# Fixed engine orders from one plan, padded feature buffers scaled by one GpSimd operation, and later query products in a fused linear-attention and gated-MLP kernel

## The chip, the cores and the metric

One core of a Trainium2 chip. The metric is the device time of one execution in microseconds (us). Medians are quoted, and the traces, whose spans are shorter than the device time by 1.7 us, decide where a microsecond went.

## The reference, cut to what matters

```python
x = A_x                                   # 1 x 2048 x 640, bf16
xn = layernorm(x)
q, k, v = split(xn @ wqkv)                # 32 heads of 20
phi_q = concat(softmax(q @ w_phi), softmax(-(q @ w_phi)))     # 40 features per head
phi_k = ...the same of k
kv, z = sum over s of phi_k * v, sum over s of phi_k          # per head
attn = (phi_q @ kv) / (phi_q @ z + 1e-6) @ wo
gated = (silu(xn @ w1) * (xn @ w3)) @ w2                      # F = 1536
return x + attn + gated
```

The kernel works on 16 tiles of 128 rows in 4 chunks. For every key or query tile TensorE projects (L431/L432 below), ScalarE takes exp of +p and -p, VectorE sums per head (reduction) and inverts (reciprocal), and the exponentials are scaled by the inverse (the *feature product*). A gate/up unit is two TensorE products into two banks of PSUM (the memory into which TensorE writes), a tanh on ScalarE, the gate operation `gs = (tanh + 1) * gate` on VectorE, which frees a bank, a copy of the up product on ScalarE and a last product on GpSimd.

## The kernel before

A small list scheduler, `Plan`, works out an order from assumed durations. Before the change only the first part was emitted in that order; the rest went through the framework's own scheduler, held by pins.

```python
def features(t, key, engines):            # before; cut
    ...
    def tail():                           # heads 30 and 31, on VectorE
        pinned[key, t] = nc.vector.tensor_mul(
            out=box["phi"][:, NB - 1, :, 0 : 2 * Dh]..., in0=box["e"][:, :, n * Dh : D]..., in1=box["r"][:, :, n:H, None]...)
    for sgn, eng in enumerate(engines):   # heads 0 to 29, +p and -p: two operations of 600 elements
        def mul(sgn=sgn, eng=eng):
            (nc.vector if eng == "DVE" else nc.gpsimd).tensor_mul(out=box["phi"][:, 0 : NB - 1, sgn, ...], ...)
...
def ln_stats(t, k=None, parts=(0, 1)):    # k: the operation that it must follow
...
b = plan.op("DVE", dve_us(512), gs, deps=[a, ab["gs"]], frees=[ug, ab["th"]])      # gate operation
...
for t in range(4, 8):
    ln_stats(t, ("g", 0, t - 2))          # statistics of chunk 1 behind gate operations
...
    if 8 <= t < 15:
        Q(t - 8)                          # query tiles 0..6 beside the key tiles
KV(NST - 2)
fill(2.2)                                 # one gate/up unit
KV(NST - 1)                               # last key/value product
...
order = plan.run()
with tc.manual_schedule(engines=...):
    ...                                   # first part only
kv_constants()
for o in order:                           # the rest: framework's scheduler, SyncE pinned
    if o["n"] >= early:
        ins = o["fn"]()
        ...
```

The softmax here doesn't subtract the row's maximum and nothing guards it: scores larger than these inputs give would overflow.

## Time and profile before

| | before |
|---|---|
| device time, median (all 6 runs before the prediction) | 274.4 us (274.02 to 276.53) |
| span in the trace | 272.65 us |
| TensorE at its own pace | 260.26 us |
| TensorE lost: start-up (first 14 us) / 20 to 27 us / gate banks 27 to 135 us / end of keys / after 145 us | 4.64 / 0.28 / 2.56 / 1.10 / 0 us |
| after the last matmul | 2.73 us |

How to read it: TensorE's matmuls have a fixed pace by shape (512 columns 0.216 us, 320 columns 0.136 us), so whatever lies between two matmul starts beyond the pace is lost time, and the span is pace, losses and the two ends. A *gate-bank* loss is a wait of TensorE for a bank that a gate operation frees late. The prediction shows the lines.

### The profile page before, as it was taken

The numbers are of one execution on the slowest core, as the hardware profiler recorded it, in microseconds if no ns is written. First come the engines' busy times: TensorE is split into PE (matmuls) and PEld (weight loads), VectorE is DVE, ScalarE is ACT, GpSimd is POOL, SyncE is SP. The second block draws the span as 40 slices with busy tenths as digits, with TensorE's granted clock in tenths as the row PEclk, the third lists the DMA queues.
The fourth block names the chain that finished last, engine by engine and source line by source line (L and its number), as shares of the span: only waits on it lengthen the run. The fifth ranks groups of instructions, "written<-read, shape, count | busy, mean of one in ns | idle before, by whom it ended". The sixth has DMA issues, their size and how long they took to land.

```text
span 272.6 us, 5218 instructions
## 1 busy us (share of the span) xinstructions
PE 264.9 (97%) x1964; PEld 164.2 (60%) x1964; DVE 184.8 (68%) x347; ACT 126.9 (47%) x285; POOL 138.9 (51%) x154
## 2 busy tenths in 40 slices
PE   7999999899999998999989999999999999999995
PEld 2545555455555665666645577766665765657775
DVE  5525899976866999799997828876567563444321
ACT  3668676557667776677754404233234133121000
POOL 6133567994568576988885422434632553112000
PEclk9999999999999999999999999999999999999999
DMA  7999927700280016706169456289814746412251
GB/s 197 312 220 306 255 80 177 268 2 0 96 99 0 2 54 172 209 37 174 68 162 331 117 137 169 103 222 288 206 49 145 168 144 188 115 50 64 82 73 48
DMA packets 70265, 38.11 MB, mean 140 GB/s; under 512 B 49632, under 2 KB 68192, under 8 KB 70240
## 3 DMA queue, kind: packets, MB, share of 16 engines
q1 hardware_dynamic: 69664, 37.42, 51.4%
q10 hardware_dynamic: 576, 0.36, 0.5%
q8 instruction: 15, 0.25, 0.4%
q14 instruction: 10, 0.08, 0.1%
HBM read 12.81 MB, written 12.98 MB: 95 GB/s over the span
## 4 chain that ended last, share of the span: by engine, by line
PE 77%; DVE 13%; issue 4%; DMA 2%; ACT 2%; SPq 0%; ACTq 0%; DVEq 0%
PE bank L633 30%; PE bank L798 19%; PE bank L432 16%; PE bank L811 8%; DVE xn L339 2%; DVE ks L490 2%; DMA wv<-in_A_wqkv_dram 2%; PE rtbank L708 2%; DVE gs L654 2%; DVE qs L490 2%; DVE stats L294 1%; PE bank L590 1%; DVE kr L501 1%; ACT ek L481 1%; DVE phi_124 L507 1%
## 5 line engine op out<-in xcount | busy, mean ns | idle before, releaser
L677 POOL TENSOR_TENSOR hT<-gs,up 128x512 bf16<-128x512 bf16 x48 | 56.1, 1171 | 77.1 <-DVE gs L654 30.2
L633 PE MATMUL bank<-xnT,w_107 128*128 128x512 bf16 x240 | 59.6, 379 | 2.1 <-DVE gs L654 2.1
L633 PE MATMUL bank<-xnT,w_108 128*128 128x512 bf16 x240 | 59.6, 379 | 0.0
L432 PEld LDWEIGHTS <-xnT 128*128 128x128 bf16 x480 | 45.8, 98 | 21.0 <-issue 1.0
L798 PE MATMUL bank<-w_109,hT 128*128 128x320 bf16 (+2 forms) x396 | 55.0, 295 | 0.0
L798 PEld LDWEIGHTS <-hT 128*128 128x128 bf16 x396 | 38.2, 98 | 15.7
L649 ACT ACTIVATE th<-bank 128x512 bf16<-128x512 f32 x48 | 28.7, 599 | 39.8 <-PE bank L633 39.8
L654 DVE SCALAR_TENSOR_TENSOR gs<-th,bank 128x512 bf16<-128x512 bf16 x48 | 32.5, 678 | 19.4 <-ACT th L649 18.9
L481 ACT ACTIVATE eq<-bank 128x320 bf16<-128x320 f32 x64 | 22.9, 439 | 44.1 <-PE bank L432 33.7
L633 PEld LDWEIGHTS <-w_108 128*128 128x128 bf16 x240 | 23.5, 98 | 28.3
L672 ACT ACTIVATE up<-bank 128x512 bf16<-128x512 f32 x48 | 28.7, 597 | 25.0 <-PE bank L633 25.0
L633 PEld LDWEIGHTS <-w_107 128*128 128x128 bf16 x240 | 22.9, 98 | 24.1 <-issue 2.8
L490 DVE TENSOR_REDUCE qs<-eq 128x64 f32<-128x1280 bf16 x16 | 23.7, 1482 | 12.0 <-ACT eq L481 12.0
L490 DVE TENSOR_REDUCE ks<-ek 128x64 f32<-128x1280 bf16 x16 | 23.6, 1473 | 8.7 <-ACT ek L481 8.7
L432 PE MATMUL bank<-wv,xnT 128*128 128x320 bf16 x160 | 24.7, 299 | 0.8 <-DMA wv<-in_A_wqkv_dram 0.7
L811 PE MATMUL bank<-wo,oT 128*128 128x320 bf16 (+2 forms) x165 | 24.6, 294 | 0.0
L432 PE MATMUL bank<-wkphi,xnT 128*128 128x320 bf16 x160 | 24.3, 299 | 0.0
L432 PE MATMUL bank<-wqphi,xnT 128*128 128x320 bf16 x160 | 24.3, 299 | 0.0
L737 DVE TENSOR_SCALAR den<-rtbank 128x18 f32<-128x18 f32 (+1 forms) x32 | 4.9, 173 | 27.9 <-PE rtbank L708 27.9
L481 ACT ACTIVATE ek<-bank 128x320 bf16<-128x320 f32 x64 | 23.0, 439 | 0.6 <-PE bank L432 0.4
L825 DVE TENSOR_TENSOR res<-bank,xr 128x320 bf16<-128x320 f32 (+2 forms) x33 | 14.5, 470 | 10.4 <-PE bank L811 10.4
L811 PEld LDWEIGHTS <-oT 128*128 128x128 bf16 x165 | 14.9, 97 | 4.9
(117 smaller groups left out, 264.9 us busy)
## 6 DMA issues: line engine op xcount, KB each, us to landing
xr<-in_A_x_dram SPq DMA_DIRECT2D x4, 640.0 KB, 6.1
out_dram<-res SPq DMA_DIRECT2D x15, 160.0 KB, 2.5
w_107<-in_B_w_dram SPq DMA_DIRECT2D x4, 480.0 KB, 6.7
w_108<-in_B_w_dram SPq DMA_DIRECT2D x4, 480.0 KB, 7.5
w_109<-in_B_w_dram SPq DMA_DIRECT2D x1, 1920.0 KB, 8.4
xg<-in_A_x_dram SPq DMA_DIRECT2D x9, 160.0 KB, 4.0
wv<-in_A_wqkv_dram SPq DMA_DIRECT2D x2, 400.0 KB, 5.8
wo<-in_A_wo_dram SPq DMA_DIRECT2D x1, 800.0 KB, 5.5
```

Source lines behind the costliest of these rows:

```text
L339: ins = nc.vector.tensor_scalar(out=xn[c][:, i, :], in0=xg[c][:, i, :], scalar1=mv[:, t, 0:1], scalar2=rstd[:, t : t + 1], op0=ALU.subtrac ...
L432: nc.tensor.matmul(o["ps"][:], xnT[:, c, t * P : (t + 1) * P], w[:, c, 320 * half : 320 * half + 320], start=(c == 0), stop=(c == KD - 1),)
L481: nc.scalar.activation(out=box["e"][:, sgn, 320 * half : 320 * half + 320], in_=o["ps"][:], func=AF.Exp, scale=1.0 - 2.0 * sgn,)
L490: nc.vector.reduce_sum(out=box["s"][:].rearrange("p a h -> p (a h)"), in_=box["e"][:].rearrange("p a (h d) -> p (a h) d", d=Dh), axis=AX.X,)
L633: nc.tensor.matmul(o["ps"][:], w[:, k, fi * P : (fi + 1) * P], xs[:, k, :], start=(k == 0), stop=(k == KD - 1))
L649: nc.scalar.activation(out=box["th"][:], in_=og["ps"][:], func=AF.Tanh, scale=0.5)
L654: pinned["g", c, fi] = nc.vector.scalar_tensor_tensor(out=box["gs"][:], in0=box["th"][:], scalar=1.0, in1=og["ps"][:], op0=ALU.add, op1=AL ...
L672: nc.scalar.activation(out=box["up"][:], in_=ou["ps"][:], func=AF.Copy, scale=0.5)
L677: lambda: nc.gpsimd.tensor_mul(out=hT[c][:, fi, :], in0=box["gs"][:], in1=box["up"][:]),
L798: nc.tensor.matmul(o["ps"][:], hT[c][:, fi, ti * P : (ti + 1) * P], w2[:, fi, lo:hi], start=(fi == 0), stop=False,)
L811: nc.tensor.matmul(o["ps"][:], oT[c][:, k, ti * P : (ti + 1) * P], wo_of[0][:, k, lo:hi], start=False, stop=(k == KD - 1),)
L825: nc.vector.tensor_tensor(out=box["res"][:, lo:hi], in0=o["ps"][:], in1=xr[c][:, ti, lo:hi], op=ALU.add)
```

## The change

Its intent: take small work off VectorE (the tails), halve the number of GpSimd feature products, fix the order of every engine by a plan that also models the SBUF port shared by VectorE and GpSimd, and place query products, attention and residual loads later.

```diff
+exps = [acts.tile([P, 2, HB * NB, Dh], bf, ...) for i in range(4)]     # padded to 33 heads, pads zero
+recs = [acts.tile([P, 2, HB * NB], f32, ...) for i in range(2)]
 # features()
-        def tail(): ...                                    # two heads on VectorE
-        for sgn, eng in enumerate(engines): def mul(...)   # 2 x 600 elements
+        muls = [plan.op("POOL", 2.5, mul(0, 2, nc.gpsimd), ...)]            # 1320 elements, one operation
+        # key tiles 14 and 15: one operation of 1320 on VectorE
 # Plan
+            done = (max(t, port) if o["port"] else t) + o["dur"]
+            if o["port"]:
+                port = done
 # gate operation
-        b = plan.op("DVE", dve_us(512), gs, ...)
+        b = plan.op("DVE", dve_us(512), gs, ..., soon=0.4)   # taken up to 0.4 us ahead of its turn
 # five gate/up units: last product on VectorE
-        return "POOL"
+        return "DVE" if 22 <= n < 32 and n % 2 else "POOL"
-        ln_stats(t, ("g", 0, t - 2))
+        ln_stats(t)
-        if 8 <= t < 15:
+        if 8 <= t < 14:
             Q(t - 8)
     KV(NST - 2)
+    Q(6)
     fill(2.2)
     KV(NST - 1)
 # last stage: RT, ATT, OT (attention of a tile) and residual loads placed later (cut)
-    kv_constants()
-    ...                                                    # framework's scheduler
+        kv_constants()
+        for o in order:                                    # whole kernel in the plan's order
+            if o["n"] >= early:
+                o["fn"]()
```

The change also alters the plan's assumptions for a few operations (the landing of the second chunk's load from 19.0 to 21.5 us, some durations, and an advance such as the gate's for two other operations).

More of the change, by code (lines that the diff above doesn't have):

```diff
@@ L17, in __init__, with op @@
         self.ops = []
-    def op(self, eng, dur, fn, deps=(), takes=None, frees=(), after=0.0, lat=0.0, soon=0.0):
+    def op(self, eng, dur, fn, deps=(), takes=None, frees=(), after=0.0, lat=0.0, soon=0.0, port=False):
         o = dict(eng=eng, dur=dur, fn=fn, deps=[d for d in deps if d is not None], takes=takes,
-                 frees=list(frees), after=after, lat=lat, soon=soon, n=len(self.ops), end=None, open=0)
+                 frees=list(frees), after=after, lat=lat, soon=soon, port=port or eng == "POOL", n=len(self.ops), end=None, open=0)
         for f in o["frees"]:
@@ L36, in run @@
         left = len(self.ops)
+        port = 0.0
         def ready(o):
@@ L66, in run @@
                 ring.remove(min(ring))
-            o["start"], o["end"] = t, t + o["dur"] + o["lat"]
-            free[o["eng"]] = t + o["dur"]
+            done = (max(t, port) if o["port"] else t) + o["dur"]
+            if o["port"]:
+                port = done
+            o["start"], o["end"] = t, done + o["lat"]
+            free[o["eng"]] = done
             queue[o["eng"]].remove(o)
@@ L151 @@
     phis = [acts.tile([P, NB, 2, 64], bf, name=f"phi{i}") for i in range(5)]
+    exps = [acts.tile([P, 2, HB * NB, Dh], bf, name=f"exp{i}") for i in range(4)]
+    recs = [acts.tile([P, 2, HB * NB], f32, name=f"rec{i}") for i in range(2)]
     kva, kvb = (kvpool.tile([P, 512], f32, name=n, tag="kv", bufs=2) for n in ("kva", "kvb"))
@@ L247, in kv_constants @@
             nc.gpsimd.memset(phi[:, :, :, HB * Dh : 64], 0.0)
-            nc.gpsimd.memset(phi[:, NB - 1, :, 2 * Dh : HB * Dh], 0.0)
+        for e in exps:
+            nc.gpsimd.memset(e[:, :, H:, :], 0.0)
+        for r in recs:
+            nc.gpsimd.memset(r[:, :, H:], 0.0)
         for q in range(2):
@@ L253, in kv_constants @@
         )
-    pinned = {}
     pin_of = {}
-    def order_after(ins, other):
-        tc.add_manual_dep(
-            ins.ins, other.ins.name,
-            mybir.DependencyInfo(mybir.DependencyClass.NoSync, mybir.DependencyReason.DATA), reason="order",
-        )
     plan = Plan(dict(bank=6, five=4, half=2, pair=4, phi=5, om=4, kv=2, th=3, gs=3, up=3, hT=3, big=3))
@@ L277 @@
     rstd = consts.tile([P, NST], f32, name="rstd")
-    arrive = [2.2, 2.6, 3.0, 3.4] + [19.0] * 4
+    arrive = [2.2, 2.6, 3.0, 3.4] + [21.5] * 4
     stats_of = {}
@@ L293, in fn @@
             for h in parts:
-                ins = nc.vector.bn_stats(out=stats[:, t, h, :], in_=xg[c][:, i, h * 320 : (h + 1) * 320])
-                if k is not None:
-                    order_after(ins, pinned[k])
+                nc.vector.bn_stats(out=stats[:, t, h, :], in_=xg[c][:, i, h * 320 : (h + 1) * 320])
             if parts[-1] == 1:
@@ L338, in fn @@
         def fn():
-            ins = nc.vector.tensor_scalar(
+            nc.vector.tensor_scalar(
                 out=xn[c][:, i, :], in0=xg[c][:, i, :], scalar1=mv[:, t, 0:1], scalar2=rstd[:, t : t + 1],
@@ L342, in fn @@
             )
-            if k is not None:
-                order_after(ins, pinned[k])
-        apply_of[t] = plan.op("DVE", 0.5, fn, deps=[rstd_of[t], *deps], frees=[xg_of[c]])
+        apply_of[t] = plan.op(
+            "DVE", dve_us(D, 4), fn, deps=[rstd_of[t], *deps], frees=[xg_of[c]], port=True, soon=1.5 if c == 1 else 0.0
+        )
         return apply_of[t]
@@ L369, in LN_out @@
             "SP", 0.5,
-            lambda: [nc.sync.dma_start(out=xn_d[c][:].rearrange("(t p) d -> p t d", p=P), in_=xn[c][:])],
+            lambda: nc.sync.dma_start(out=xn_d[c][:].rearrange("(t p) d -> p t d", p=P), in_=xn[c][:]),
             deps=ds, frees=[a], lat=3.5,
@@ L374, in tr @@
         def tr():
-            pinned["xnT", c] = ins = nc.sync.dma_start_transpose(
+            nc.sync.dma_start_transpose(
                 out=xnT[:, :, 512 * c : 512 * c + 512], in_=xn_d[c][:]
             )
-            return [ins]
         xt = plan.op("SP", 2.5, tr, deps=[st], lat=3.0)
@@ L462, in features @@
         box = {}
-        exps = []
+        done = []
         w, ready = (wkphi, wphi_ready["k"]) if key == "k" else (wqphi, wphi_ready["q"])
         def al():
-            box["e"] = work.tile([P, 2, D], bf, name="e" + key, tag="pair", bufs=4)
+            box["e"] = exps.pop(0)
+            exps.append(box["e"])
         def alp():
@@ L481, in ex @@
                     nc.scalar.activation(
-                        out=box["e"][:, sgn, 320 * half : 320 * half + 320], in_=o["ps"][:],
-                        func=AF.Exp, scale=1.0 - 2.0 * sgn,
+                        out=box["e"][:, sgn, 16 * half : 16 * half + 16, :],
+                        in_=o["ps"][:].rearrange("p (h d) -> p h d", d=Dh), func=AF.Exp, scale=1.0 - 2.0 * sgn,
                     )
-                exps.append(plan.op("ACT", act_us(320), ex, deps=[u, ea], frees=[u]))
+                done.append(plan.op("ACT", act_us(320), ex, deps=[u, ea], frees=[u]))
@@ L488, in red @@
         def red():
             box["s"] = small.tile([P, 2, H], f32, name=key + "s", tag="ks", bufs=2)
-            nc.vector.reduce_sum(
-                out=box["s"][:].rearrange("p a h -> p (a h)"),
-                in_=box["e"][:].rearrange("p a (h d) -> p (a h) d", d=Dh), axis=AX.X,
-            )
-        last = plan.op("DVE", dve_us(2 * D), red, deps=exps)
-        pa = plan.alloc("phi", alp)
-        muls = []
-        def rec():
-            box["r"] = small.tile([P, 2, H], f32, name=key + "r", tag="kr", bufs=2)
-            nc.vector.reciprocal(out=box["r"][:], in_=box["s"][:])
@@ L503, in features @@
-        last = plan.op("DVE", dve_us(2 * H, 0.15), rec, deps=[last])
-        n = HB * (NB - 1)
-        def tail():
-            pinned[key, t] = nc.vector.tensor_mul(
-                out=box["phi"][:, NB - 1, :, 0 : 2 * Dh].rearrange("p a (h d) -> p a h d", d=Dh),
-                in0=box["e"][:, :, n * Dh : D].rearrange("p a (h d) -> p a h d", d=Dh),
-                in1=box["r"][:, :, n:H, None].to_broadcast([P, 2, H - n, Dh]),
-            )
-        muls.append(plan.op("DVE", dve_us(2 * (H - n) * Dh), tail, deps=[last, pa], frees=[ea]))
@@ L514, in features @@
-        for sgn, eng in enumerate(engines):
-            def mul(sgn=sgn, eng=eng):
-                (nc.vector if eng == "DVE" else nc.gpsimd).tensor_mul(
-                    out=box["phi"][:, 0 : NB - 1, sgn, 0 : HB * Dh].rearrange("p b (h d) -> p b h d", d=Dh),
-                    in0=box["e"][:, sgn, 0 : n * Dh].rearrange("p (b h d) -> p b h d", h=HB, d=Dh),
-                    in1=box["r"][:, sgn, 0:n, None]
-                    .to_broadcast([P, n, Dh])
-                    .rearrange("p (b h) d -> p b h d", h=HB),
-                )
-            muls.append(
-                plan.op(eng, dve_us(n * Dh) if eng == "DVE" else 1.22, mul, deps=[last, pa], frees=[ea])
-            )
+            nc.vector.reduce_sum(out=box["s"][:], in_=box["e"][:, :, 0:H, :], axis=AX.X)
@@ new lines, in features, with rec, mul, fn @@
+        last = plan.op("DVE", dve_us(2 * D), red, deps=done)
+        def rec():
+            box["r"] = recs.pop(0)
+            recs.append(box["r"])
+            nc.vector.reciprocal(out=box["r"][:, :, 0:H], in_=box["s"][:])
+        last = pin_of[key, t] = plan.op("DVE", dve_us(2 * H, 0.15), rec, deps=[last])
+        pa = plan.alloc("phi", alp)
+        def mul(at, n, eng):
+            def fn():
+                eng.tensor_mul(
+                    out=box["phi"][:, :, at : at + n, 0 : HB * Dh].rearrange("p b a f -> p a b f"),
+                    in0=box["e"][:, at : at + n].rearrange("p a (b h) d -> p a b (h d)", h=HB),
+                    in1=box["r"][:, at : at + n, :, None].to_broadcast([P, n, HB * NB, Dh]),
+                )
+            return fn
@@ new lines, in features @@
+        if engines == ("DVE", "DVE"):
+            muls = [plan.op("DVE", dve_us(1320), mul(0, 2, nc.vector), deps=[last, pa], frees=[ea], port=True)]
+        elif engines[1] == "POOL":
+            muls = [plan.op("POOL", 2.5, mul(0, 2, nc.gpsimd), deps=[last, pa], frees=[ea])]
+        else:
+            muls = [
+                plan.op("POOL", 1.3, mul(0, 1, nc.gpsimd), deps=[last, pa], frees=[ea]),
+                plan.op("DVE", dve_us(660), mul(1, 1, nc.vector), deps=[last, pa], frees=[ea], port=True),
+            ]
@@ L528, in features @@
         return muls, pa, box
     def K(t):
-        phik_of[t], phik_a[t], _ = features(t, "k", ("POOL", "POOL" if t < NST - 1 else "DVE"))
-        pin_of["k", t] = phik_of[t][0]
+        phik_of[t], phik_a[t], _ = features(t, "k", ("POOL", "POOL") if t < NST - 2 else ("DVE", "DVE"))
     def Q(t, engines=("POOL", "POOL")):
@@ L567, in fn @@
                 )
-        KV_of[t] = plan.op("PE", pe_us(NB, 63), fn, deps=phik_of[t] + V_of[t], frees=[phik_a[t]])
+        KV_of[t] = plan.op("PE", 0.032 * NB, fn, deps=phik_of[t] + V_of[t], frees=[phik_a[t]])
     FSPANS = (
@@ L653, in gs @@
         def gs():
-            pinned["g", c, fi] = nc.vector.scalar_tensor_tensor(
+            nc.vector.scalar_tensor_tensor(
                 out=box["gs"][:], in0=box["th"][:], scalar=1.0, in1=og["ps"][:], op0=ALU.add, op1=ALU.mult
             )
-        b = plan.op("DVE", dve_us(512), gs, deps=[a, ab["gs"]], frees=[ug, ab["th"]])
+        b = plan.op("DVE", dve_us(512), gs, deps=[a, ab["gs"]], frees=[ug, ab["th"]], soon=0.4)
         pin_of["g", c, fi] = b
@@ L692, in fn @@
                 )
-            kvm_of.append(plan.op("DVE", dve_us(63 * (b1 - b0)), fn, deps=[KV_of[NST - 1]]))
+            kvm_of.append(plan.op("DVE", dve_us(63 * (b1 - b0)), fn, deps=[KV_of[NST - 1]], soon=1.0))
     rt_of = {}
@@ L714, in RT @@
             u = plan.op(
-                "PE", pe_us(b1 - b0, 63), fn, deps=[kvm_of[half], pqT_of[pair]], takes="kv", frees=[pqT_a[pair]]
+                "PE", 0.032 * (b1 - b0), fn, deps=[kvm_of[half], pqT_of[pair]], takes="kv", frees=[pqT_a[pair]]
             )
@@ L989 @@
             gates[0][0]()
+        if t < 2:
+            RT(t + 3)
+            ATT(t + 3)
+            OT(t + 3)
+        if t == 0:
             gates[1][0]()
@@ L992 @@
             gates[t][0]()
-        if t + 3 < NST:
-            if t % 4 == 1:
-                residual(t // 4 + 1)
-            RT(t + 3)
-            ATT(t + 3)
-            OT(t + 3)
         gates[t][1]()
@@ L1001 @@
             Q(t + 8)
+        if t % 4 == 3 and t < NST - 1:
+            residual(t // 4 + 1)
+        for n in (t + 3,) if 1 < t < 9 else (t + 4,) if 8 < t < 12 else ():
+            RT(n)
+            ATT(n)
+            OT(n)
         if 3 <= t < 11:
             fill(1.5 * 2.16)
+        if t == 8:
+            RT(12)
+            ATT(12)
+            OT(12)
         if t == 10:
@@ L1013 @@
             o["fn"]()
-    kv_constants()
-    queued = None
-    for o in order:
-        if o["n"] >= early:
-            ins = o["fn"]()
-            if o["eng"] == "SP":
-                for ins in ins:
-                    if queued is not None:
-                        order_after(ins, queued)
-                    queued = ins
+        kv_constants()
+        for o in order:
+            if o["n"] >= early:
+                o["fn"]()
     kvpool.release()
```

## The prediction

> **What bounds the kernel now.** First the page: busy time by engine and the rows of forty slices.
>
> ```profile
> PE 264.9 (97%) x1964; PEld 164.2 (60%) x1964; DVE 184.8 (68%) x347; ACT 126.9 (47%) x285; POOL 138.9 (51%) x154
> ...
> PE   7999999899999998999989999999999999999995
> ...
> DVE  5525899976866999799997828876567563444321
> ...
> PEclk9999999999999999999999999999999999999999
> ```
>
> TensorE is busy in every slice at full granted clock, so it is the bound, and the span can only shrink where it waits. A busy TensorE may still crawl, so I checked its pace in the chain of waits: ten 512-column matmuls take 2.16 us and ten 320-column ones 1.36 us, the same in every stage; outside the start-up no stretch is slower. Adding up matmul starts at that pace leaves 3.7 us lost after the first 25 us of the 272.6 us span. The waits view, TensorE alone, names it:
>
> ```profile
> PE bank L633 <- DVE gs L654: 2.1, 3, 0.8
> PE kva L562 <- DVE phi_125 L517: 0.9, 1, 0.9
> PE bank L220 <- PEq L1036: 0.8, 1, 0.8
> PE bank L432 <- DMA wv<-in_A_wqkv_dram: 0.7, 1, 0.7
> ```
>
> The first two rows are the change's target: a gate/up product waits three times for a PSUM bank that VectorE frees late (at 48, 53 and 106 us), and the last key/value product once for the last key features (142 us). They sum to 3.0 us here; start-to-start spacing gives 0.96 + 0.68 + 0.92 + 1.10 = 3.66 us, because the view ends a matmul about 0.16 us after the next could have started. I use 3.66. The last two rows belong to the first 8 us, which the change leaves alone.
>
> Why VectorE is late shows in the busy time by stretch: at three of the four stalls it is full.
>
> ```profile
> 30.00:54.00 24.00, 22.69 (x146) 12.34 (x144) 22.94 (x38) 16.27 (x37) 18.01 (x17) 1.00 0.63 191
> ...
> 85.00:108.00 23.00, 22.24 (x180) 14.43 (x178) 20.50 (x24) 17.28 (x43) 15.19 (x15) 1.00 0.17 55
> ```
>
> Columns: the stretch, its length, busy PE, weight loads, DVE, ACT, POOL. VectorE has 22.9 of 24.0 us; from 90 to 108 us it never pauses. The timeline of VectorE and GpSimd at 89 us shows what fills it:
>
> ```profile
> 89.98 1.15 POOL L677 TENSOR_TENSOR hT<-gs,up 128x512 bf16<-128x512 bf16 x1 [1.77 <-DVE gs L654]
> 90.21 1.10 DVE L339 TENSOR_SCALAR xn<-xg,mv,rstd 128x640 bf16<-128x640 bf16 x1
> 91.09 2.45 POOL L517 TENSOR_TENSOR phi_126<-ek,kr 128x600 bf16<-128x600 bf16 x2
> 91.23 1.24 DVE L507 TENSOR_TENSOR phi_126<-ek,kr 128x80 bf16<-128x80 bf16 x1
> 92.39 1.32 DVE L339 TENSOR_SCALAR xn<-xg,mv,rstd 128x640 bf16<-128x640 bf16 x1
> ```
>
> An 80-element product takes 1.24 us and a layernorm scaling 1.10 or 1.32 us, while the fastest of their groups take 0.24 and 0.39 us; each slow one ends as a GpSimd operation ends.
>
> **What the Trainium skill says.** "SBUF — State Buffer", section "Who interferes with whom": the SBUF port pair that VectorE and GpSimd share is an exclusive lock for a whole instruction; a VectorE operation with two SBUF inputs contends with a GpSimd one that reads SBUF, tensor_scalar in a two-port mode too, tensor_reduce on trn2 never. The trace agrees: L507 and L339 stretch, the 1280-element reductions stay at 1.47 to 1.49 us. "Perfetto Trace Analysis", section "Identifying the Most-Contended Engine", warns that matmul busy time is no measure of distance to the roofline; hence the check by pace. "GPSIMD Engine Reference", section 2.1, gives about 2.5 cycles per element as the floor of a two-input operation, at 1.2 GHz. The trace's 600 elements in 1.20 us are 2.4, near it; I use the trace.
>
> **The change, part by part.**
>
> *Padded buffers, one GpSimd operation.* Gone: 32 two-head tails on VectorE (L507, 27.8 us by stretch, 0.87 each) and 63 GpSimd products of 600 elements (1.20 each, 75.9 us). New: 30 GpSimd products of 1320 elements. Two rows of the trace, 600 elements in 1.20 and 800 in 1.53 us, extrapolate to 2.4; proportional growth gives 2.6. I take 2.5, 75 us in all: GpSimd neither wins nor loses. The last two key tiles go to VectorE, 1320 elements each, about 1.5 us by the rate of the reduction (1280 in 1.48), less one old 1.78 us operation: +1.2.
>
> *Five gate/up units with the last product on VectorE.* 5 x 0.68 = 3.4 us more on VectorE (as L654), 5 x 0.6 less on ScalarE, 5 x 1.17 less on GpSimd. VectorE: 184.8 - 27.8 + 1.2 + 3.4 = 161.6, perhaps 159 with fewer blocked scalings. Per key tile its load falls by 0.87 us, so both stretches above get slack: of a 6.57 us period with a query and a key tile, two reductions (2.96), two reciprocals (1.04), one or two L654-like operations (0.68 to 1.36) leave 1.2 to 1.9 us. The three bank waits should go: **-2.56 us**.
>
> *The end of the keys.* In the built program the query product of tile 6 and a gate/up unit now stand between the last key projection and the last key/value product: 7.7 us instead of 6.3. VectorE's chain for it (reduction, unit, reciprocal, product, a possible port wait of 1.2) comes to about the same. I allow 0.3 us left of 1.10: **-0.8 us**.
>
> *Later query products, later residual loads.* They move 0.33 us groups (L708) behind others in a stage without any TensorE wait. The closest lead I found: the product of tile 5 now precedes its use by 11.7 us (3.26 + 1.36 + 1.36 + 0.33 + 2.16 + 3.26); evacuation 2, store 2.4, transposes queued 4, landing 3.8 or less need about 9.5. The residual of tile 4 may land 2 us late, yet its bank is needed 3.8 us later. **0**, if DMA keeps its times.
>
> *Fixed orders: a loss.* Formerly each layernorm statistic of the second chunk stood behind a named gate operation; now the plan decides. In the built program VectorE runs gate 1, gate 2, statistics of tile 4, gate 3, statistics of 5 and of 6, gate 4. Formerly gate 3 came before statistics 4, and only one statistic stood between gates 3 and 4. The timeline before:
>
> ```profile
> 20.75 0.69 DVE L654 SCALAR_TENSOR_TENSOR gs<-th,bank 128x512 bf16<-128x512 bf16 x1 [1.47 <-ACT th L649]
> 21.67 0.89 DVE L294 BATCH_NORM_STATS2 stats<-xg 128x6 f32<-128x320 bf16 x2 [0.24 <-DMA xg<-in_A_x_dram]
> 22.55 1.24 PE L633 MATMUL bank<-xnT,w_108 128*128 128x512 bf16 x5
> 23.45 0.69 DVE L654 SCALAR_TENSOR_TENSOR gs<-th,bank 128x512 bf16<-128x512 bf16 x1 [0.65 <-ACT th L649]
> 24.05 0.88 DVE L294 BATCH_NORM_STATS2 stats<-xg 128x6 f32<-128x320 bf16 x2
> ```
>
> The statistics wait for a load that lands at 21.67. An in-order VectorE now holds gate 3 until 21.67 + 1.13 = 22.80, done at 23.45; the matmul group at 22.55 needs that bank (its semaphore in the built program is gate 3), so it starts at 23.5. Then two statistics, 2 x 1.13, and gate 4 ends at 26.4; the fifth weight-product group after it, at 24.47 before, needs that bank: TensorE is 1.9 us behind. The 0.28 us it lost there before are inside. **+1.65 us**; nothing later gives it back, as TensorE has no slack.
>
> Sum: -2.56 - 0.8 + 1.65 + 0.3 for small waits not found = -1.4. 274.4 - 1.4 = **273.0 us**.
>
> **The rivals.** *R1, no early loss:* the load lands sooner, or TensorE finds the banks; then only the gains count, about 271. For it: the plan's author moved the assumed landing to 21.5, so knew of it. Against: the order in the built program and the 21.67. *R2, GpSimd becomes the bound of the middle stage:* one long operation holds the port 2.5 us where two of 1.2 let VectorE in between; reciprocals wait for the recs buffer two features back. If scalings block for 2.5 us each (four do at 90 to 108 us), VectorE is up to 5 us late against a slack of about 2 per period; 1 to 3 us lost, 274 to 276. Against: GpSimd's load there is 5.0 + 0.6 of 6.57 us per period. *R3, late transposes or residuals* in the last 100 us: 11.7 us of lead against 9.5 is thin; 1 to 2 us more, 274 to 275. *R4, hidden anyway:* VectorE's relief of 23 us is worth at most 3.66, since TensorE's 1964 matmuls stay the same; this I hold certain, and it caps the gain at 1.3%.
>
> **Range and chances.** R1 sets the low side, 270.5; R2 or R3 on top of the sum the high side, 275.5. Faster by over 2% needs 268.9, below the cap: 0.02. Slower by over 2% needs 279.9, a stall of 7 us that I do not see: 0.03. Within 2%: 0.95.
>
> **What would show it.** Right: no TensorE wait on the gate operation at 48, 53 and 106 us; TensorE waits near 22.6 and 24.5 us, 1.5 to 2 us together, on L646; VectorE about 160 us; L504 about 2.5 us each; a matmul pace unchanged. Wrong: no wait at 22 to 27 us (R1), new waits on L646, L656 or L504 between 85 and 145 us (R2), waits on oT or xr after 150 us (R3), or a different pace of TensorE, which would break the cap.

## The result, and the profile after

The changed kernel takes 271.97 us median (271.65 to 274.49, 10 runs), the kernel before, run beside it, 274.33 us (273.96 to 276.93, 20 runs). The ratio is 0.9912, 95% interval 0.9879 to 0.9945: within 2%. Ratios are the mean time of one kernel's fast runs over that of the other's of the same rounds, so not quite the ratio of the medians quoted here.

The page of the changed kernel, parts 1 and 2:

```profile
PE 263.7 (98%) x1964; PEld 164.0 (61%) x1964; DVE 168.6 (62%) x321; ACT 124.3 (46%) x280; POOL 131.5 (49%) x117
...
PE   7998999999999999999999999999999999999995
```

VectorE fell from 184.8 to 168.6 us, and TensorE's row has a single 8 left, in the fourth slice (20.2 to 27.0 us), where the kernel before has three later ones. The waits view of TensorE of the changed kernel:

```profile
PE bank L431 <- DMA wv<-in_A_wqkv_dram: 0.9, 2, 0.6
PE bank L226 <- PEq L1032: 0.8, 1, 0.8
PE bank L582 <- DVE gs L646: 0.7, 1, 0.7
PE bank L405 <- DVE xn L339: 0.3, 1, 0.3
PE bank L625 <- DVE gs L646: 0.3, 1, 0.3
```

The 2.1 us on the gate operation and the 0.9 us on the last key features are gone; what is left on `gs` are two new waits, both over by 25.2 us. The same two stretches as in the prediction (length, then busy PE, weight loads, DVE, ACT, POOL):

```profile
30.00:54.00 24.00, 24.00 (x155) 13.23 (x154) 18.84 (x33) 16.83 (x37) 18.32 (x12) 1.00 0.62 183
...
85.00:108.00 23.00, 23.00 (x173) 14.55 (x172) 20.26 (x21) 16.27 (x41) 14.95 (x10) 1.00 0.25 73
```

TensorE is full in both; VectorE fell from 22.94 to 18.84 us in the first, but hardly in the second. The timeline of the changed kernel at 20 to 25 us has the new waits:

```profile
20.85 0.89 DVE L296 BATCH_NORM_STATS2 stats<-xg 128x6 f32<-128x320 bf16 x2 [2.01 <-DMA xg<-in_A_x_dram]
...
21.90 0.63 DVE L646 SCALAR_TENSOR_TENSOR gs<-th,bank 128x512 bf16<-128x512 bf16 x1
...
22.58 1.24 PE L625 MATMUL bank<-xnT,w_108 128*128 128x512 bf16 x5 [0.30 <-DVE gs L646]
...
24.48 0.64 DVE L646 SCALAR_TENSOR_TENSOR gs<-th,bank 128x512 bf16<-128x512 bf16 x1
...
25.17 0.47 PE L582 MATMUL bank<-wphi,wkT 128*128 128x80 bf16 x6 [0.72 <-DVE gs L646]
```

VectorE stands before the statistics until their load lands at 20.85 us, and the gate operation whose bank TensorE needs stands behind it. By start-to-start spacing TensorE loses 0.47 us there and 0.88 us at the second.

The sum of the differences: gate banks -2.56, end of keys -1.10, early 1.35 - 0.28 = +1.07, start-up 4.22 instead of 4.64 = -0.42, after the last matmul 3.08 instead of 2.73 = +0.35; together -2.66, and the spans differ by 272.65 - 270.00 = 2.65 us. I put the last two down to chance. The first gate/up product starts at 14.09 us after and 14.52 us before, but over all the traces, whose first stage has the same order, it starts anywhere from 14.09 to 14.84 us, and the time after the last matmul is 2.7 to 2.8 us in all traces but three, the changed kernel's among them, where it is 3.06 to 3.08, with the same instructions last.

### The profile page after: what moved, and what is told of

The parts are those of the page before. It is cut to its first block, busy times and chain, and to the rows that moved or that the text cites. A ratio compares the mean times of both kernels' runs of the same rounds, so it can differ in the third digit from the quotient of the medians.

```text
span 270.0 us, 5107 instructions
## 1 busy us (share of the span) xinstructions
PE 263.7 (98%) x1964; PEld 164.0 (61%) x1964; DVE 168.6 (62%) x321; ACT 124.3 (46%) x280; POOL 131.5 (49%) x117
## 4 chain that ended last, share of the span: by engine, by line
PE 90%; SPq 5%; DMA 2%; DVE 2%; issue 0%
PE bank L625 35%; PE bank L431 22%; PE bank L790 19%; PE bank L803 8%; SPq L195 2%; PE rtbank L700 2%; DMA xg<-in_A_x_dram 2%; SPq L171 2%; PE kva L554 1%; DVE stats L296 1%; PE kvb L554 1%; PE bank L582 1%; SPq L193 0%; DVE gs L646 0%; SPq L174 0%
## 5 line engine op out<-in xcount | busy, mean ns | idle before, releaser
L669 POOL TENSOR_TENSOR hT<-gs,up 128x512 bf16<-128x512 bf16 x43 | 49.8, 1158 | 80.6 <-ACT up L664 40.0
L817 DVE TENSOR_TENSOR res<-bank,xr 128x320 bf16<-128x320 f32 (+2 forms) x33 | 15.8, 478 | 38.6 <-PE bank L803 38.6
L664 ACT ACTIVATE up<-bank 128x512 bf16<-128x512 f32 x43 | 25.7, 597 | 22.9 <-PE bank L625 21.9
L803 PEld LDWEIGHTS <-oT 128*128 128x128 bf16 x165 | 15.8, 98 | 5.8
L481 ACT ACTIVATE exp_128<-bank 128x320 bf16<-128x320 f32 x32 | 11.5, 435 | 13.1 <-PE bank L431 13.0
L481 ACT ACTIVATE exp_131<-bank 128x320 bf16<-128x320 f32 x32 | 11.5, 437 | 12.3 <-PE bank L431 12.3
L296 DVE BATCH_NORM_STATS2 stats<-xg 128x6 f32<-128x320 bf16 x32 | 13.8, 468 | 4.7 <-DMA xg<-in_A_x_dram 4.7
L481 ACT ACTIVATE exp_129<-bank 128x320 bf16<-128x320 f32 x32 | 11.6, 434 | 10.7 <-PE bank L431 10.7
L481 ACT ACTIVATE exp_130<-bank 128x320 bf16<-128x320 f32 x32 | 11.5, 438 | 10.1 <-PE bank L431 10.1
```

Source lines behind the costliest of these rows:

```text
L296: nc.vector.bn_stats(out=stats[:, t, h, :], in_=xg[c][:, i, h * 320 : (h + 1) * 320])
L481: nc.scalar.activation(out=box["e"][:, sgn, 16 * half : 16 * half + 16, :], in_=o["ps"][:].rearrange("p (h d) -> p h d", d=Dh), func=AF.Ex ...
L664: nc.scalar.activation(out=box["up"][:], in_=ou["ps"][:], func=AF.Copy, scale=0.5)
L669: lambda: nc.gpsimd.tensor_mul(out=hT[c][:, fi, :], in0=box["gs"][:], in1=box["up"][:]),
L803: nc.tensor.matmul(o["ps"][:], oT[c][:, k, ti * P : (ti + 1) * P], wo_of[0][:, k, lo:hi], start=False, stop=(k == KD - 1),)
L817: nc.vector.tensor_tensor(out=box["res"][:, lo:hi], in0=o["ps"][:], in1=xr[c][:, ti, lo:hi], op=ALU.add)
```

## The experiments

All gave right results. The runs were made in three groups, each with the kernel before beside them: runs 1 to 4 below; tb_soon0, soon0, q6_back and end_back; and tb_soon0_again, tb_plain, plain and end_q6_back. The first group ran on another chip than the other two. The table gives the time and TensorE's losses by place, from start-to-start spacing in the run's one trace; the experiments follow. In four traces (1938 of 1964 matmul records) a missing record shows as a gap of exactly one matmul, and these gaps are taken out.

| run | median us | ratio to before | 20-27 us | gate banks, 27-135 | end of keys | after 145 |
|---|---|---|---|---|---|---|
| before | 274.33 | 1 | 0.28 | 2.56 | 1.10 | 0 |
| changed | 271.97 | 0.9912 | 1.35 | 0 | 0 | 0 |
| gates_first | 271.21 | 0.9886 | 0.28 | 0 | 0 | 0 |
| tail_back | 271.99 | 0.9929 | 1.23 | 0 | 0 | 0 |
| before_padded | 272.66 | 0.9926 | 0.28 | 0.43 | 1.57 | 0 |
| two_ops | 271.68 | 0.9892 | 1.28 | 0 | 0 | 0 |
| tb_soon0 | 274.24 (three runs) | 0.9971 | trace unusable | | | |
| tb_soon0_again | 274.01 (one run) | - | 1.27 | 2.35 | 0 | 0 |
| soon0 | 271.91 | 0.9886 | 1.33 | 0.05 | 0 | 0 |
| q6_back | 272.32 | 0.9925 | 1.36 | 0 | 0.63 | 0 |
| end_back | 274.26 | 0.9973 | 1.84 | 0 | 0 | 1.46 |
| tb_plain | 271.72 | 0.9924 | 1.28 | 0 | 0 | 0 |
| plain | 270.36 | 0.9868 | 0.28 | 0 | 0 | 0 |
| end_q6_back | 273.44 | 0.9982 | 1.31 | 0 | 0.63 | 0.98 |

The kernel before took 274.29, 274.46 and 274.0 us median in the three groups.

### 1. gates_first: what the freed statistics cost

```diff
     for t in range(4, 8):
-        ln_stats(t)
+        ln_stats(t, ("g", 0, t - 2))
```

> The changed kernel, with each layernorm statistic of the second chunk again behind a named gate operation (gate 3 now precedes the statistics of tile 4, one statistic between any two gates). My theory (the fixed order of gates and statistics costs TensorE 0.47 us at 21.9 and 0.88 us at 24.2, where the kernel before lost 0.28): both losses on L646 between 20 and 27 us shrink to 0.3 or less in sum, the time falls by about 1.0 us against the changed kernel, to 270.9 (ratio to the kernel before 0.9875). Rival (TensorE is slowed there by something else, such as the load of w1/w3 or the gate banks themselves): the losses stay over 1 us and the time stays within 0.3 of 272.0. Second rival (the later statistics delay the second chunk's transposes, and the loss returns at 30 to 45 us): the time stays at 272 with a new TensorE wait on xnT or L339.

271.21 us (ratio 0.9886, interval 0.9846 to 0.9926). The early losses are back at the 0.28 us of the kernel before, and none comes later. The timeline of this run has the gate operation ahead of the statistics:

```profile
20.61 0.69 DVE L646 SCALAR_TENSOR_TENSOR gs<-th,bank 128x512 bf16<-128x512 bf16 x1 [1.47 <-ACT th L641]
20.86 0.64 PE L582 MATMUL bank<-wphi,wkT 128*128 128x140 bf16 x9
21.21 0.88 DVE L296 BATCH_NORM_STATS2 stats<-xg 128x6 f32<-128x320 bf16 x2
```

So the order of gates and statistics costs 1.35 - 0.28 = 1.07 us, as my theory had it. The median gained 0.76 us rather than 1.0. The two traces' spans differ by 0.80 us: this trace's first gate/up product starts 0.29 us later than the changed kernel's, which is in the range of chance named above. Whether that holds for the medians isn't shown.

### 2. tail_back: is it VectorE's relief?

```diff
-  padded exps and recs, one GpSimd product of 1320 elements
+  features() and the zeroing of the kernel before: tails on VectorE, 2 x 600 elements on GpSimd
   (plan, port model, gate soon=0.4, Q(6), last stage stay as changed)
```

> The changed kernel with the feature product of the kernel before: 32 two-head tails on VectorE, two GpSimd products of 600 elements per tile, no padding; plan, port model and all placements stay as changed. My theory (VectorE's relief, not the order, removed the bank waits): VectorE busy time up by 20 to 28 us to 190 or more, TensorE loses 1.5 to 3 us on L646-like operations or key features between 40 and 145 us, time 273.5 to 275. Rival (a fixed order that knows the port is enough): under 0.3 us of TensorE loss after 25 us, time within 0.4 of 272.0.

My theory fell. VectorE's busy time is back at 186.9 us, and yet TensorE loses nothing between 27 and 145 us; 271.99 us median. The relief was not needed for the bank waits to go. The rival, that the fixed order is enough, holds.

### 3. before_padded: is the relief enough by itself?

```diff
  kernel before, its scheduler, pins and placement
+ padded exps and recs, one GpSimd product; key tiles 14 and 15: one VectorE product
```

> The kernel before (its scheduler, its pins, its plan without the port, its query placement) with only the padded buffers and the one GpSimd product; the last two key tiles have one VectorE product each. My theory: the three bank waits at 48, 53 and 106 us go (-2.6 us); the early loss stays at 0.3; of the 1.10 us at the end of the keys I do not know how much stays, since query tile 6 is still ahead. Time 271.2 to 272.2, so as fast as the changed kernel. Rival (the fixed orders carry the gain): 273.5 to 274.5, with TensorE waits on the gate operation still over 1.5 us in sum after 40 us.

272.66 us, 0.5 us slower than my range. The three bank waits of 2.56 us are gone, with one of 0.43 us at 134 us instead. The relief is not quite alone here: at 48 and 53 us the gate operation still stands behind the statistics, but near 106 us the framework's scheduler now put it ahead of the second reciprocal (102.56 against 103.10 us), so there its place changed with the relief; run 6 is the cleaner case for that wait. What missed is the end of the keys, 1.57 us instead of 1.10. VectorE's timeline there:

```profile
130.28 3.49 DVE L510 TENSOR_TENSOR phi<-exp,rec 128x1320 bf16<-128x1320 bf16 x1
...
138.12 3.48 DVE L510 TENSOR_TENSOR phi<-exp,rec 128x1320 bf16<-128x1320 bf16 x1
```

The GpSimd product that began at 129.95 us runs 2.43 us, to 132.38; the VectorE product that began at 130.28 ends at 133.77, 1.39 us after it, while a free one takes 1.52 us. The gate operation behind it, at 133.69 us, is the one for which TensorE loses the 0.43 us. The product before the last key/value product suffers the same behind a GpSimd product from 137.78 us. A product moved to VectorE only helps where the GpSimd is quiet.

### 4. two_ops: one long operation or two short ones?

```diff
-  muls = [plan.op("POOL", 2.5, mul(0, 2, nc.gpsimd), ...)]
+  muls = [plan.op("POOL", 1.3, mul(n, 1, nc.gpsimd), ...) for n in range(2)]
```

> The changed kernel with the padded product split in two GpSimd operations of 660 elements, padding kept and no tail on VectorE. My theory (what helps is that VectorE's tail is gone; one operation or two is beside the point, and a long one holds the shared port no worse than two short ones): GpSimd operations of 1.30 us each, time within 0.3 us of the changed kernel's 272.0. Rival (one long operation matters, for better): 0.5 us or more slower, with new TensorE waits after 80 us; or (for worse, port held 2.5 us at once): 0.3 us or more faster with L339 scalings shorter than the 865 ns mean.

271.68 us, and the losses of the changed kernel (1.28 us against 1.35, all early): as expected, no difference. One sign of the second rival did come: the layernorm scalings (L339) took 761 ns on average, not 865; TensorE gained nothing from it. The groups view of this run, then of the changed kernel (busy us and mean ns after the bar):

```profile
L504 POOL TENSOR_TENSOR phi<-exp,rec 128x660 bf16<-128x660 bf16 x60 | 77.3, 1313 | 20.6 <-DVE rec L497 9.2 <-ACT exp L481 8.6 <-ACT vaug L445 2.2
```

```profile
L504 POOL TENSOR_TENSOR phi_127<-exp_129,rec_133 128x1320 bf16<-128x1320 bf16 x2 | 4.9, 2426 | 3.5 <-DVE rec_133 L497 3.5
```

Two of 1.31 us take GpSimd 0.2 us longer per tile than one of 2.43.

### 5. tb_soon0 and tb_soon0_again: the gate's place

The kernel of tail_back has as full a VectorE as before and no waits. Its timeline shows the gate operation ahead of the two reductions where the kernel before had it behind two reductions, two reciprocals and a tail, and TensorE behind it:

```profile
106.67 0.68 DVE L654 SCALAR_TENSOR_TENSOR gs<-th,bank 128x512 bf16<-128x512 bf16 x1
...
107.40 1.24 PE L633 MATMUL bank<-xnT,w_107 128*128 128x512 bf16 x5 [0.76 <-DVE gs L654]
```

So the new theory: what counts is the gate's place in the queue.

```diff
  kernel of tail_back
-        b = plan.op("DVE", dve_us(512), gs, deps=[a, ab["gs"]], frees=[ug, ab["th"]], soon=0.4)
+        b = plan.op("DVE", dve_us(512), gs, deps=[a, ab["gs"]], frees=[ug, ab["th"]])
```

> The kernel of the run tail_back (changed kernel, feature product of the kernel before with its VectorE tails), and in its plan the gate operation no longer taken 0.4 us ahead of its turn. Its VectorE order from 90 us on is then two reductions, two reciprocals, two tails, gate, as in the kernel before, instead of reduction, gate, reciprocal. Theory formed on tail_back: what removed the bank waits there is the gate's place in VectorE's fixed order, as VectorE was just as full (186.9 us); so the waits return: 1.0 to 2.5 us lost by TensorE on the gate operation between 85 and 110 us, time 272.4 to 274. Rival (the port model, the five units with the product on VectorE or the fixed order as such are enough): under 0.3 us lost after 27 us, time within 0.4 of tail_back's 271.4 fast runs.

The three timed runs took 273.73 to 274.44 us, but the profiled execution took 984 us with matmuls at about a quarter of their pace although the listed clock is 1.0; in the same group one run of the kernel before took 465 us, at a listed clock of 0.56. I do not know why, and drew nothing from that trace. The kernel ran once more:

> The same kernel as the run tb_soon0, of which three timed runs took 273.7 to 274.4 us but whose one profiled execution took 984 us, TensorE at about a quarter of its pace from start to near the end, so that its trace cannot be read. Theory as then (the gate's place in VectorE's order): 1.5 us or more lost by TensorE on L648 between 85 and 135 us, behind two reductions, two reciprocals and two tails. Rival: the 2.7 us come from elsewhere, for example a late oT or pqT transpose after 145 us, and there is under 0.3 us on L648 between 27 and 140.

274.01 us (one run, its state unknown, its clock 0.999; before 274.0), and waits on the gate are back: 0.99 us at 98 and 1.36 us at 107 us. VectorE's timeline ahead of the second, and the TensorE group that waits:

```profile
101.57 1.47 DVE L484 TENSOR_REDUCE qs<-eq 128x64 f32<-128x1280 bf16 x1
102.97 1.47 DVE L484 TENSOR_REDUCE ks<-ek 128x64 f32<-128x1280 bf16 x1
104.36 0.54 DVE L495 RECIPROCAL qr<-qs 128x64 f32<-128x64 f32 x1
104.82 0.49 DVE L495 RECIPROCAL kr<-ks 128x64 f32<-128x64 f32 x1
105.23 1.11 DVE L501 TENSOR_TENSOR phi<-eq,qr 128x80 bf16<-128x80 bf16 x1
106.27 1.24 DVE L501 TENSOR_TENSOR phi<-ek,kr 128x80 bf16<-128x80 bf16 x1
107.43 0.68 DVE L648 SCALAR_TENSOR_TENSOR gs<-th,bank 128x512 bf16<-128x512 bf16 x1
```

```profile
108.15 2.10 PE L627 MATMUL bank<-xnT,w 128*128 128x512 bf16 x9 [1.20 <-DVE gs L648]
```

Here the gate operation is last of seven; in tail_back the same one, the 25th, came first:

```profile
101.53 0.67 DVE L648 SCALAR_TENSOR_TENSOR gs<-th,bank 128x512 bf16<-128x512 bf16 x1
102.12 1.47 DVE L484 TENSOR_REDUCE qs<-eq 128x64 f32<-128x1280 bf16 x1
```

The busy time by stretch of the two kernels, tail_back first, says that it is the place and not the amount of work:

```profile
85.00:108.00 23.00, 22.84 (x170) 14.51 (x172) 21.29 (x24) 16.24 (x41) 13.94 (x14) 1.00 0.20 63
```

```profile
85.00:108.00 23.00, 21.12 (x163) 13.51 (x161) 20.82 (x23) 16.11 (x41) 13.63 (x14) 1.00 0.20 62
```

VectorE is busier (21.29 against 20.82 of 23 us) in the kernel that loses nothing. The PE figure of the first is short of 23.00 by missing records. The Trainium skill says on "PSUM — Partial Sum Buffer", section "Engine vs sequencer instructions", that the queues of ScalarE, VectorE and GpSimd are strict FIFO; this trace agrees: the tanh that the gate operation needs ended at 102.10 us, and it still ran at 107.43 us, behind five operations that began later than 102.10. In tb_soon0_again nothing is lost at 48 and 53 us, so this edit brought back one of the three old waits and made a new one at 98 us; at 48 us the plan's order had the gates ahead of the statistics even so (47.40 against 48.00 us), where the kernel before had the statistics first (47.49 against 48.29).

### 6. soon0: the gate's place where the tails are gone

```diff
  changed kernel
-        b = plan.op("DVE", dve_us(512), gs, ..., soon=0.4)
+        b = plan.op("DVE", dve_us(512), gs, ...)
```

> The changed kernel with the gate operation no longer taken 0.4 us ahead of its turn; padded buffers stay. Theory: without the tails VectorE has enough slack that the gate's place is of no account, as in the run before_padded: under 0.3 us of TensorE loss between 27 and 140 us, time within 0.4 of the changed kernel's. Rival (the gate's place is what counts with or without tails): 0.7 us or more lost on L646 between 85 and 110 us.

271.91 us and no loss after 27 us but one of 0.05 us at 106, as expected. With runs 2, 3 and 5 this fills the square: of the two, tails gone or gate early, either is enough, and only with neither are the gate-bank waits there (2.56 in the kernel before, 2.35 us in tb_soon0_again, not at all the same places). Both work on one quantity, how long after its tanh a gate operation starts. For the 25th it is 4.89 us in the kernel before and 5.33 in tb_soon0_again, where TensorE loses 0.92 and 1.36 us; 0.79 in tail_back, where it loses nothing; and 4.07 here, behind two reductions and two reciprocals but no tail, where it loses 0.05. So TensorE bears about 4 us at this place, and this run only just stays under it.

### 7. q6_back: the end of the keys

```diff
-        if 8 <= t < 14:
+        if 8 <= t < 15:
             Q(t - 8)
     KV(NST - 2)
-    Q(6)
     fill(2.2)
```

> The changed kernel with query tile 6 back ahead of key tile 15, as in the kernel before. Theory (prediction's step on the end of the keys: the query product between the last key projection and the last key/value product hides VectorE's chain for the last key tile): TensorE waits 0.8 to 1.6 us on the last key/value product near 140 us, on phi L504, and the time rises by as much, to 272.8 to 273.4. Rival (the chain is shorter for another reason, one VectorE product in place of two by two engines): under 0.3 us there, time as the changed kernel's.

272.32 us; the wait is back, 0.63 us, smaller than the 0.8 that I gave as its least. TensorE's timeline:

```profile
141.11 0.36 PE L554 MATMUL kva<-vaug,phi 128*128 128x63 bf16 x6 [0.47 <-DVE phi L504]
```

So the query product between the last key projection and the last key/value product hides VectorE's chain, but 0.47 of the former 1.10 us went by something else in the change: the single VectorE product or the fixed order. No run takes these apart, but before_padded has the single product without the fixed order and loses 1.57 us, so the product alone isn't it: there it stood behind a GpSimd product and took 3.48 us, while in q6_back it starts ahead of one (138.98 against 139.62 us) and takes 2.07.

### 8. end_back and end_q6_back: the last stage

```diff
  changed kernel (end_back); with the edit of run 7 as well (end_q6_back)
-  RT, ATT, OT of tile t+3 behind the attention product of tile t; residual(t // 4 + 1) at t % 4 == 3
+  RT, ATT, OT of tile t+3 ahead of it; residual(t // 4 + 1) at t % 4 == 1
```

> The changed kernel with the last stage placed as in the kernel before: RT, ATT and OT of tile t+3 ahead of the attention product of tile t, residual loads one tile earlier. Theory (prediction's step: this move is worth 0): TensorE loses under 0.3 us after 145 us and the time is within 0.3 us of the changed kernel's. Rival (the later placement is needed, since the query products move too): 0.5 us or more lost on oT, pqT, xr or an rtbank after 145 us.

I was wrong: 274.26 us, with a new wait in the last stage. (Its early loss is also 0.5 us larger, because its load landed late; see below.)

```profile
170.58 1.53 PE L803 MATMUL bank<-wo,oT 128*128 128x320 bf16 x10 [1.31 <-DMA oT<-od]
```

I then thought that only the later query tile 6, whose store goes the same way, made this so:

> The changed kernel with the last stage placed as in the kernel before (the run end_back, which lost 1.46 us at 169 us on the transpose oT) and query tile 6 back ahead of key tile 15 (the run q6_back, which lost 0.63 us at 140 us on the last key product). Theory (the later last stage is only needed because query tile 6 and its store moved later): the wait on oT near 169 us is gone or under 0.3 us, 0.4 to 0.9 us stay at the end of the keys, time 272.2 to 272.8. Rival (the early placement of RT, ATT, OT is too tight by itself under the fixed order): 1 us or more lost on oT near 169 us, time 274 or more.

That fell too: 0.98 us of the 1.46 stay, and 273.44 us. The early placement is too tight by itself once TensorE reaches that point sooner: the group that waits was due at 169.07 us here and at 170.88 us in the kernel before, while the transpose that it needs was issued at 166.58 against 165.73 us. VectorE's chain isn't why the issue is 0.85 us later: the attention rows (`om`) that the transpose needs were ready at 161.26 us here and at 162.97 in the kernel before. But their store was issued at 163.90 us (163.30 before), right behind a transpose of query features that SyncE's queue held from 160.92 to 163.77 us (159.69 to 162.78 before). So the delay is in SyncE's queue; why that earlier transpose came later stays open.

### 9. tb_plain and plain: the port model and the five units

```diff
  kernel of tail_back (tb_plain), kernel of gates_first (plain)
-                 ... port=port or eng == "POOL", ...
+                 ... port=False, ...
-        return "DVE" if 22 <= n < 32 and n % 2 else "POOL"
+        return "POOL"
```

> The kernel of the run tail_back (VectorE tails as before, fixed orders, gate taken 0.4 us sooner) with a plan that does not know the port and with all gate/up units' last product on GpSimd. Theory (the gate's place alone removes the bank waits): under 0.3 us of TensorE loss on gate operations between 27 and 140 us, time within 0.4 us of tail_back's fast runs, 271.4. Rival (port model or the five units on VectorE carry part): 0.7 us or more lost between 85 and 140 us.

271.72 us, no loss between 27 and 145 us: neither the port model nor the five units carry any of it, even with the tails there.

> The kernel of the run gates_first (changed kernel, statistics behind named gates again) with a plan that does not know the port and with all gate/up units' last product on GpSimd. Theory (neither is worth anything once the tails are gone): no TensorE loss over 0.2 us after 14 us, time within 0.3 of gates_first's 271.2. Rival (the port knowledge or the five units are needed): 0.5 us or more lost between 85 and 145 us on L646, L504 or kva.

270.36 us, ratio 0.9868, interval 0.9853 to 0.9882: the lowest median, without the port model and the five units. No single loss after 14 us is over 0.2 us, and its trace span of 269.07 us is that of gates_first (269.20), so these two traces show no gain. The 0.85 us between the medians stay unexplained: the groups ran on different chips, and the traced run is the slowest of plain's four and the fastest of gates_first's six. Nor did the port model shorten what it was for. The groups view of gates_first and of plain, which differ in the port model and the five units alone, mean ns after the bar's comma:

```profile
L339 DVE TENSOR_SCALAR xn<-xg,mv,rstd 128x640 bf16<-128x640 bf16 x16 | 13.4, 866 | 0.1
```

```profile
L339 DVE TENSOR_SCALAR xn<-xg,mv,rstd 128x640 bf16<-128x640 bf16 x16 | 12.2, 785 | 0.1
```

The scalings, which contend with GpSimd for the port, took 806 ns on average before, 866 with the port in the plan and 785 without; with the tails it is 754 (tail_back) and 712 (tb_plain). These are small sums, 1.3 and 0.7 us over 16 scalings.

## Why the prediction was right or wrong

The time, 273.0 predicted and 271.97 measured, was in the range and within 2% as forecast; the gain was 2.4 us where 1.4 was predicted. By its steps:

1. **TensorE is the bound and its losses cap the gain.** Right. The pace is unchanged at 260.26 us, and no run gained more than its losses allow. The best run took away all of the 3.66 us and gained 3.6 us by its medians.
2. **Padded buffers take the three bank waits away, -2.56.** The size was exact, the reason half right, and as the change holds a second cause that is enough by itself, the exact size is no evidence for the first. Relief is sufficient (soon0, and before_padded but for 0.43 us) but was not necessary (tail_back, tb_plain): the gate's earlier place in VectorE's order does it as well, and the prediction did not name it. The prediction read "VectorE has 22.9 of 24.0 us" as the cause; tail_back shows that a VectorE with the tails, with 21.29 of 23 us at 85 to 108 us, stalls nobody when the gate is ahead. The costs were near: GpSimd products 2.43 us (2.5 predicted). VectorE's busy time is 168.6 us, not 160, for the most part through an error of reckoning: the prediction took durations (27.8 us of tails) off a busy time, in which the overlap of neighbouring instructions counts once. The sum of VectorE's durations fell from 204.1 to 182.1 us, by 22.0, near the 23.2 of its working; the busy time fell by 16.2. Of the rest, the scalings were not fewer blocked but more (13.8 us in durations against 12.9), and the two VectorE products took 3.94 us, not 3.0, as one met the port. (The reductions that it gives as 1.47 to 1.49 us ran 1.43 to 1.49.)
3. **End of the keys, -0.8 with 0.3 left.** Right direction, -1.10: nothing was left, as VectorE's product ended at 139.51 us, 0.8 us ahead of the matmul that needs it at 140.29. q6_back shows that 0.63 us of it is the moved query product.
4. **Later query products and last stage, 0.** The net is 0 as predicted, but not because the placement is idle: undone within the changed kernel it costs 1.46 us (end_back). The prediction compared it with a stage that had no wait and did not ask whether that stage would keep its slack when TensorE came sooner. Its closest lead is also summed wrongly: 2, 2.4, 4 and 3.8 us make 12.2 and not 9.5, which is more than the lead of 11.7, so that unless they overlap, which it doesn't say, its own figures did not give 0.
5. **The early loss, +1.65.** The mechanism is right to the instruction (gate 3 behind the statistics, then gate 4 behind two more; gates_first removes both); the size was too large, +1.07. The term mis-sized is the landing of the load. In all nine traces with this order, the first loss equals the landing of the load, less the start of the first gate/up product, less 6.29 us, within 0.01: 6.63 gives 0.34 (tail_back), 6.76 gives 0.47 (changed), 7.25 gives 0.96 (end_back). Before, the difference was 7.15, which would give 0.86; the prediction had 0.95. The load landed sooner in the changed kernel's trace, and as far as the traces show that is chance: it is issued behind the wkT transpose in SyncE's queue, which took 6.28 us in the trace of the kernel before and 6.34 in end_back, but 5.79 to 5.82 in the other eleven, before_padded among them. So the prediction rested on one trace with an uncommonly late load; even so the landing explains 0.39 of the 0.58 us, and the rest is small overestimates in the chain. The second loss was 0.88 or 0.89 us in every such trace, and the prediction had 1.9 - 0.95 = 0.95.
6. **0.3 for small waits.** None appeared.

The rivals: R1 (no early loss, about 271) did not happen, but the version with it removed lands there. R2 (GpSimd's long operation blocks VectorE): the mechanism is there, as one scaling took 2.54 us in the changed kernel, but it costs nothing, and two_ops shows that the length of the operation is of no account to TensorE here. R3 (late transposes) is what end_back brings about. R4's cap holds.

What failed in the sum is the early term by 0.58 us, the key term by 0.30, the small waits by 0.30: -1.4 predicted, -2.6 from the change.

## What to carry to other kernels

When TensorE waits for a buffer that a secondary engine frees, look first at what stands ahead of the freeing operation in that engine's queue; moving it forward was worth as much here as removing 25 us of work from that engine (the tails as tail_back shows them, 13.9 + 11.4 us), and doing both gained nothing more. An operation that waits for a load must not stand ahead of one that frees a bank, or the landing time of the load goes into the total one for one (the relation in step 5). After stalls are removed, check the later stages again: a placement that had slack before may be what TensorE now runs into.

## What the Trainium skill lacked or had wrong

- "Perfetto Trace Analysis", section "Identifying the Most-Contended Engine", goes by occupancy for VectorE. It lacks, as does the page's advice on bubbles that VectorE causes, that an engine which isn't the bound acts by its order: VectorE at 21.29 of 23 us cost TensorE nothing, at 20.82 of 23 us 2.35 us.
- "GPSIMD Engine Reference", section 2.1, calls about 2.5 cycles per element a floor for two inputs. Taken by start-to-start spacing, 1320 elements took 2.39 us here (112.25 to 114.64 us in the changed kernel), which at its 1.2 GHz is 2.17 cycles per element with all overhead in it; so it is not a floor for these operands, one of which is broadcast.
- "SBUF — State Buffer", section "Who interferes with whom", agrees with the runs (a VectorE product of 1.52 us took 3.49 us behind a GpSimd product, and ended 1.39 us after it). It lacks a hint that planning around the lock may be worth nothing: with a port model in the plan (gates_first) the scalings took 866 ns, without it (plain) 785, with no TensorE wait on the gates after 27 us in either.
- No page has it: the same loads at the start of the kernel land up to 0.77 us apart from trace to trace (the statistics that wait for one start at 8.46 to 9.23 us, the first gate/up product at 14.09 to 14.84), which in a 270 us kernel is as large as most effects told here.
